# An attention, MLP and routed-expert kernel: the current token's term on TensorE, the key products on VectorE, the routing's counts one gap later

## The chip, the cores and the metric

The kernel runs on one core of a Trainium2 chip. The metric is the device time of one execution in microseconds (us): a median over runs without the profiler.

## What is computed

Three parts follow one another: an attention with a decaying state, an MLP with a squared ReLU, and a layer of 8 experts of which each token takes the best one, up to a capacity. B=2, H=8, S=768, D=48; so 1536 tokens of 384 numbers, all in float32.

```python
for t in range(S):                                   # attention, per (batch, head)
    cur = einsum('bhd,bhe->bhde', u[None] * kt, vt)  # the current token's term
    y[:, :, t] = einsum('bhd,bhde->bhe', rt, state + cur)
    state = wt[..., None] * state + einsum('bhd,bhe->bhde', kt, vt)
x = y as (tokens, 384)
x = square(maximum(x @ w_in, 0)) @ w_out             # MLP, d_ff = 2048
logits = x @ w_gate                                  # routing to 8 experts
expert, gate = argmax(logits), softmax(logits) at the argmax
slot = number of earlier tokens with the same expert # dropped if slot >= 384
out = gate * (maximum(x @ w1[expert], 0) @ w2[expert])
```

The term `cur` gives each token t and head h the vector v[t] times one number, the sum over d of r[t,d] * u[d] * k[t,d]. This sum is what the change computes in another way.

## The kernel before

**Attention** (function `attention`, class `Chunk`). The tokens go in 12 chunks of 128; chunks 0 to 5 are the first batch, 6 to 11 the second. Within a chunk, the heads go as four pairs: w, k and r lie with the head dimensions on the partitions (two heads of 48, each padded to 64) and 4 x 128 tokens along the row. v lies with the tokens on the partitions. The methods of a chunk, in the order of the mathematics:

- `suffix` (line 256) and `prefix` (276): scans of the decays on VectorE, from the chunk's end and from its start; `total` (270, 271) sets the prefix scan's first element.
- `keys` (264) multiplies k with the suffix scan, `queries` (282) r with the prefix scan. Which engine does it is set by chunk in the tables `KEYS_V` (2, 3, 4, 8 on VectorE) and `QUERIES_V` (0, 3, 6), the others on GpSimd.
- `scores` (330): 8 matmuls, `causal` (338): two masks on VectorE that read them from PSUM. `turn_keys` (292): transposes and a copy on ScalarE; `outer` (346): the chunk's addition to the state; `state` (356 or 358): two sums on VectorE; `decay` (301): the state scaled, on ScalarE.
- `values` (364, 365, 368): 12 matmuls into one PSUM tile (8 in chunks 0 and 6).
- The current token's term: `load_b` loads k and r a second time, in token order (tokens on the partitions); `bonus1` (308, 309): two products on GpSimd, k * u * r; `bonus2` (314): a reduce over each head on VectorE; `bonus3` (322): GpSimd multiplies v with the sums, into y.
- `finish` (374) adds the values to y on VectorE; `turn` (384, 385) transposes y and ScalarE rounds it to `xhi`, `turn2` (388) forms the remainder `xlo` on VectorE. `check1` and `check2` are squares on ScalarE whose sums watch for overflow.

The order of the work is written out by hand: the tuple `order` lists pairs (offset, method), and round n of the loop (`for n in range(13)`) calls the method on chunk n + offset. Each engine then works through its instructions in this order. A round so holds `total` and `prefix` of chunk n+1, `suffix` and `keys` of chunk n+2, `causal`, `outer`, `state` and `values` of chunk n, `finish` and `turn` of chunk n-1. At the end of a round the loads are issued on SP's queue: w and k of chunk n+4, the others of chunk n+3. In rounds 9 to 11 the entry `conv` starts the conversion of the MLP's weights (class `Conv`; line 122 is GpSimd's part).

**MLP** (`moe1`). It runs twice: over token groups 0 and 1 (512 tokens each), then over group 2. Each float32 product is three matmuls of rounded parts (hi*hi, hi*lo, lo*hi). Step i of its loop is up (475, 9 matmuls), the square of step i-1 (481, 482), the parts of step i-2 (488, 490), then one piece of a background generator, here called a gap, then down of step i-3 (502, 9 matmuls).

**Routing** (`route_bg`). In the gaps of the second pass groups 0 and 1 are routed: four items with the logits of 128 tokens each (578), one with `choose` (591 to 600: argmax and softmax), one with `count` and `total` (605 to 610, 633, 634: matmuls that count earlier tokens of the same expert), one with `slots`, `gates` and the first `send` (619 to 628, 656: the token's row to its expert's slot in DRAM), then three more with a `send` each. `pairs` joins two items to a gap. `judge` and `early` follow (fetch and turn the first rows of expert 0, 734 and 742). The experts come last (`experts`).

Of the kernel before, what the change touches and what calls it, by code (L numbers as in the profile page):

```python
# [19 lines left out]
P = 128  # L20
# [17 lines left out]
KEYS_V = (2, 3, 4, 8)  # L38
QUERIES_V = (0, 3, 6)
# [4 lines left out]
def tile_rwkv_moe_moe2(ctx, tc, cap, rt, kt, wt, vp, rn, kn, un, wmoe, we, wg, cf, ci, fill, vt, up, ind, out, disp, xt):  # L44
# [14 lines left out]
    ub = cpool.tile([P, DM], F32, name="ub")  # L59
# [147 lines left out]
    def attention(conv):  # L207
# [7 lines left out]
        nc.vector.memset(z1, 0.0)  # L215
        st = ap1.tile([P, NPAIR, 96], F32, name="st")
# [3 lines left out]
        class Chunk:  # L220
# [25 lines left out]
            def load_b(self):  # L246
                n = self.n
                self.kn = ap2.tile([P, DM], F32, name=f"kn_{n}", tag="kn")
                nc.sync.dma_start(self.kn, kn[n * P : (n + 1) * P, :])
                self.rn = ap2.tile([P, DM], F32, name=f"rn_{n}", tag="rn")  # L250
                nc.sync.dma_start(self.rn, rn[n * P : (n + 1) * P, :])

# [65 lines left out]
            def bonus3(self):  # L318
                self.y = ylast if self.n == 11 else ap2.tile([P, NPAIR, 2, D], F32, name=f"y_{self.n}", tag="y")
# [72 lines left out]
        def do(n, *names):  # L392
# [8 lines left out]
            "ub": lambda: nc.sync.dma_start(ub, un),  # L401
# [544 lines left out]
    def run(fast):  # L946
# [163 lines left out]
```

## Time and profile before

| | us |
|---|---|
| median of 3 runs | 474.16 |
| lowest and highest | 473.64, 476.53 |
| the profiled execution | 478.65 |
| its span, first to last instruction | 476.8 |
| TensorE busy in the span | 437.2 |
| VectorE busy | 317.0 |
| ScalarE busy | 232.7 |
| GpSimd busy | 171.1 |

PE is TensorE's matmuls, DVE VectorE, ACT ScalarE, POOL GpSimd, SP the engine whose queue issues most DMAs. Ends of matmuls are modelled, so the distance between starts says more than a duration; a float32 matmul shows as two records. In rows in order of time the first number is the start in us from the span's start, the second the us of the piece, then engine, line, operation, output<-inputs, and in brackets the idle time of the engine before it and what ended it. In rows of windows the granted clock is a share of 2.4 GHz.

### The profile page before, as it was taken

The page shows a single profiled execution, that of the slowest core. Times are in us where ns is not written, and L with a number is a line of the kernel's source. Part 1 is how long each engine was busy: PE and PEld are TensorE (multiplying, and loading weights), DVE is VectorE, ACT ScalarE, POOL GpSimd, SP SyncE. Part 2 cuts the span into 40 slices and gives each one's busy share as a digit, 9 for nine tenths or more (in the row PEclk, how much of TensorE's full clock was granted, in tenths as well). Part 3 has the DMA queues.
Part 4 walks back from the last instruction along what each step waited for, and adds up shares of the span by engine and source line. Part 5 has one row for each costly group of instructions (what it writes and reads, how often), then busy time and mean ns, then how long its engine had stood idle before and what let it go on. Part 6 is the DMA issues. An engine that isn't in the chain of part 4 may idle for free. (4 is left out here: it accounts for less than half of the span.)

```text
span 476.8 us, 7070 instructions
## 1 busy us (share of the span) xinstructions
PE 437.2 (92%) x2349; PEld 368.7 (77%) x2349; DVE 317.0 (66%) x550; ACT 232.7 (49%) x477; POOL 171.1 (36%) x174
## 2 busy tenths in 40 slices
PE   3898889799999999999989999998999889989992
PEld 2797778678888888888878787786888778878882
DVE  6989999968766667765444556532279994993230
ACT  2454445656665555663343644442357663643230
POOL 3747767723212222211004260132046662561000
PEclk9989889989999999999999999998999999999998
DMA  8775766659774232333003245416139999500000
GB/s 286 251 209 200 230 203 215 212 173 329 237 239 135 87 89 90 99 101 100 1 0 100 67 133 183 133 45 221 40 94 376 308 352 335 199 6 29 16 19 16
DMA packets 35908, 73.45 MB, mean 154 GB/s; under 512 B 3884, under 2 KB 18270, under 8 KB 35728
## 3 DMA queue, kind: packets, MB, share of 16 engines
q1 hardware_dynamic: 32336, 61.02, 39.6%
q10 hardware_dynamic: 1856, 7.33, 4.4%
q0 software_dynamic: 1664, 4.47, 2.5%
q8 instruction: 25, 0.41, 0.3%
q14 instruction: 27, 0.22, 0.1%
HBM read 68.33 MB, written 12.46 MB: 169 GB/s over the span
## 5 line engine op out<-in xcount | busy, mean ns | idle before, releaser
L490 DVE TENSOR_TENSOR glo<-gg,ghi 128x512 fp32r<-128x512 f32 x48 | 35.8, 745 | 48.4 <-ACT ghi L488 48.3
L122 POOL TENSOR_TENSOR raw<-raw 128x384 int32<-128x384 int32 x32 | 30.0, 938 | 96.6 <-ACT gg L481 77.9
L488 ACT ACTIVATE ghi<-gg 128x512 fp32r<-128x512 f32 x48 | 30.3, 632 | 60.9 <-PE px L502 60.6
L774 ACT ACTIVATE place_lo<-pu 128x512 f32<-128x512 f32 x28 | 16.7, 598 | 61.2 <-PE pu L769 61.2
L808 POOL DMA_INDIRECT out_dram<-yo,drow x13 | 16.1, 1241 | 77.1 <-DVE yo L807 44.6
L785 DVE TENSOR_TENSOR place_lo<-ph,place_hi 128x512 fp32r<-128x512 f32 x28 | 18.8, 687 | 36.4 <-ACT place_hi L784 36.4
L482 DVE SCALAR_TENSOR_TENSOR gg<-ph,gg 128x512 f32<-128x512 f32 x48 | 32.9, 685 | 14.7 <-ACT gg L481 14.7
L481 ACT ACTIVATE gg<-ph 128x512 f32<-128x512 f32 x48 | 28.7, 598 | 15.8 <-PE ph L475 11.6
L365 PE MATMUL py<-v,am 128*128 128x96 f32 x96 | 22.3, 319 | 6.8 <-DVE am L338 6.8
L365 PEld LDWEIGHTS py<-v,am 128*128 128x128 f32 x96 | 17.5, 227 | 8.0 <-DVE am L338 8.0
L368 PE MATMUL py<-v,am 128*128 128x96 f32 x96 | 22.5, 322 | 1.2
L652 POOL COPY row<-sm 128x1 f32<-128x1 f32 x9 | 2.3, 256 | 58.8 <-DVE sm L628 43.4
L769 PE MATMUL pu<-e_0hi,dhi 128*128 128x512 f32 x42 | 17.6, 420 | 3.2 <-PEq L834 2.5
L802 PE MATMUL py<-e_2hi,place_hi 128*128 128x384 f32 x56 | 20.2, 361 | 0.0
L368 PEld LDWEIGHTS py<-v,am 128*128 128x128 f32 x96 | 17.7, 230 | 2.7 <-DVE am L338 2.7
L807 DVE TENSOR_SCALAR yo<-py,drow 128x384 f32<-128x384 f32 x13 | 8.0, 613 | 17.6 <-PE py L802 17.6
L256 DVE TENSOR_TENSOR_SCAN q<-w,d1r 128x516 f32<-128x516 f32 x12 | 17.6, 1468 | 2.6 <-DMA w<-wt_dram 2.6
L116 DVE SCALAR_TENSOR_TENSOR raw<-raw,cy 128x384 int32<-128x384 int32 x32 | 18.6, 581 | 1.2
L784 ACT ACTIVATE place_hi<-ph 128x512 fp32r<-128x512 f32 x28 | 16.7, 596 | 5.0 <-ACT place_hi L784 4.7
L802 PE MATMUL py<-e_2lo,place_hi 128*128 128x384 f32 x56 | 18.9, 337 | 0.0
L802 PE MATMUL py<-e_3lo,place_hi 128*128 128x384 f32 x56 | 18.8, 336 | 0.0
L802 PE MATMUL py<-e_3hi,place_hi 128*128 128x384 f32 x56 | 18.8, 336 | 0.0
(227 smaller groups left out, 1374.8 us busy)
## 6 DMA issues: line engine op xcount, KB each, us to landing
rawe<-we_dram SPq DMA_DIRECT2D x40, 384.0 KB, 4.9
raw<-wmoe_dram SPq DMA_DIRECT2D x32, 384.0 KB, 4.0
disp_dram<-fill_dram ACTq DMA_DIRECT2D x8, 606.2 KB, 5.6
place_hi<-we_dram SPq DMA_DIRECT2D x12, 384.0 KB, 8.1
v<-vp_dram SPq DMA_DIRECT2D x12, 288.0 KB, 5.1
drow<-disp_dram SPq DMA_DIRECT2D x8, 388.0 KB, 4.1
w<-wt_dram SPq DMA_DIRECT2D x12, 258.5 KB, 4.3
k<-kt_dram SPq DMA_DIRECT2D x12, 256.0 KB, 4.7
```

The costliest lines, as they stand in the source:

```text
L116: nc.vector.scalar_tensor_tensor(raw[:, :, 1], raw[:, :, 1], -0x40000000, yi, op0=ALU.bitwise_and, op1=ALU.bitwise_or)
L122: nc.gpsimd.tensor_tensor(raw[:, :, 1], raw[:, :, 1], raw[:, :, 0], op=ALU.add)
L256: nc.vector.tensor_tensor_scan(q[:, ::-1], self.w[:, NSEG * SEG : 0 : -1], d1r[:, ::-1], 0.0, op0=ALU.mult, op1=ALU.add)
L365: nc.tensor.matmul(py[:, a, :], self.at[0][:, a, :], self.vv[:, a, 0:96], start=self.first, stop=False)
L368: nc.tensor.matmul(py[:, a, :], self.at[1][:, a, :], self.vv[:, a, 48:144], start=False, stop=True)
L481: nc.scalar.activation(gg, gh[f, g], AF.Relu)
L482: nc.vector.scalar_tensor_tensor(gg, gh[f, g], 0.0, gg, op0=ALU.max, op1=ALU.mult)
L488: nc.scalar.activation(ghi, gg, AF.Copy)
L490: nc.vector.tensor_tensor(glo, gg, ghi.bitcast(F32), op=ALU.subtract)
L769: nc.tensor.matmul(p_, xx[:, kk, :], wx[:, kk, :], start=n == 0, stop=n == 8)
L785: nc.vector.tensor_tensor(hlo, p_, hhi.bitcast(F32), op=ALU.subtract)
L802: nc.tensor.matmul(py, hx[f // 4][xi][:, f % 4, :], wx, start=n == 0, stop=n == 23)
```

## The change

1. The current token's sums. `load_b` goes. GpSimd's `bonus1` is one product z = k * r in the layout of the pairs, made one round earlier (at offset 2). `bonus2` is four matmuls on TensorE (128x128 by 128x96) of z with `ub`, which now holds u on the diagonal blocks of the pairs, so that each head's sum comes out 48 times; ScalarE copies it to y, and `bonus3` is GpSimd's product of y with v. It stands behind `bonus2`, ahead of `outer`.
2. All `keys` are on VectorE; all `queries` but chunk 0's are on GpSimd.
3. `ub` is built by ScalarE from `upt` (4 numbers a partition) instead of being loaded; the slow variant `recurrence` no longer loads `upt` itself.
4. `pairs` ends a gap after every even item instead of after every odd one: the gaps hold logits 0; logits 1 and 2; logits 3 with `choose`; `count` with `slots` and the first send; and so on.

```diff
-KEYS_V = (2, 3, 4, 8)
-QUERIES_V = (0, 3, 6)
+QUERIES_V = (0,)
...
-            def load_b(self):
-                n = self.n
-                self.kn = ap2.tile([P, DM], F32, name=f"kn_{n}", tag="kn")
-                nc.sync.dma_start(self.kn, kn[n * P : (n + 1) * P, :])
-                self.rn = ap2.tile([P, DM], F32, name=f"rn_{n}", tag="rn")
-                nc.sync.dma_start(self.rn, rn[n * P : (n + 1) * P, :])
...
             def keys(self):
-                eng = nc.vector if self.n in KEYS_V else nc.gpsimd
-                eng.tensor_tensor(self.kh, self.k, self.q3[:, :, 1:SEG], op=ALU.mult)
+                nc.vector.tensor_tensor(self.kh, self.k, self.q3[:, :, 1:SEG], op=ALU.mult)
...
             def bonus1(self):
-                nc.gpsimd.tensor_tensor(self.kn, self.kn, ub, op=ALU.mult)
-                nc.gpsimd.tensor_tensor(self.kn, self.kn, self.rn, op=ALU.mult)
+                self.z = ap2.tile([P, NPAIR, P], F32, name=f"z_{self.n}", tag="z", bufs=3)
+                nc.gpsimd.tensor_tensor(self.z, self.k, self.r, op=ALU.mult)
 
             def bonus2(self):
-                n = self.n
-                self.bs = ap2.tile([P, H], F32, name=f"bs_{n}", tag="bs")
-                nc.vector.tensor_reduce(
-                    self.bs, self.kn.rearrange("p (h d) -> p h d", d=D), op=ALU.add, axis=AX.X
-                )
+                self.pb = ps.tile([P, NPAIR, 2, D], F32, name=f"pb_{self.n}", tag="misc", bufs=3)
+                for a in range(NPAIR):
+                    nc.tensor.matmul(
+                        self.pb[:, a].rearrange("p j d -> p (j d)"), self.z[:, a, :],
+                        ub[:, a].rearrange("p j d -> p (j d)"), start=True, stop=True,
+                    )
+                self.y = ylast if self.n == 11 else ap2.tile([P, NPAIR, 2, D], F32, name=f"y_{self.n}", tag="y")
+                nc.scalar.activation(self.y, self.pb, AF.Copy)
 
             def bonus3(self):
-                bsb = self.bs.rearrange("p (a j) -> p a j", j=2).unsqueeze(3).to_broadcast([P, NPAIR, 2, D])
-                nc.gpsimd.tensor_tensor(self.y, vnat, bsb, op=ALU.mult)
+                nc.gpsimd.tensor_tensor(self.y, self.y, vnat, op=ALU.mult)
...
-            (1, "total"), (0, "scores"), (-1, "finish"), (1, "turn_keys"), (1, "prefix"), (0, "causal"), (2, "suffix"), (1, "queries"), (0, "bonus2"), (0, "outer"), (2, "keys"), (-1, "turn"), (1, "check1"), (0, "state"), (0, "bonus3"), (1, "bonus1"), (1, "decay"), (0, "conv"), (0, "values"), (-1, "turn2"), (1, "check2"),
+            (1, "total"), (0, "scores"), (-1, "finish"), (1, "turn_keys"), (1, "prefix"), (0, "causal"), (2, "suffix"), (1, "queries"), (0, "bonus2"), (0, "bonus3"), (0, "outer"), (2, "keys"), (2, "bonus1"), (-1, "turn"), (1, "check1"), (0, "state"), (1, "decay"), (0, "conv"), (0, "values"), (-1, "turn2"), (1, "check2"),
...
-            do(n + 3, "load_r", "load_v", "load_b")
+            do(n + 3, "load_r", "load_v")
...
             for i, _ in enumerate(g_):
-                if i % 2:
+                if i % 2 == 0:
                     yield
```

VectorE's instructions of round 9, before; pl, p and q are the scale, the prefix scan and the suffix scan, kh the keys, am the masked scores, bs the sums of the current token, st the state, xlo the remainder of the output.

```order
L270 TENSOR_SCALAR pl_10_898<-q_845 128x4
L271 RECIPROCAL z_93<-pl_10_898 128x4
L374 TENSOR_TENSOR y_866<-py_875,y_866 128x384
L276 SCALAR_TENSOR_TENSOR p_919<-w_716,z_93 128x516
L338 TENSOR_TENSOR am_0_921<-psc_0_901,cst 128x512
L338 TENSOR_TENSOR am_1_923<-psc_1_902,cst 128x512
L256 SCALAR_TENSOR_TENSOR q_925<-w_800,d1r 128x516
L314 TENSOR_REDUCE bs_929<-kn_724 128x8
L358 TENSOR_TENSOR st<-t_870,pu_931 64x4x48 x2
L388 TENSOR_TENSOR xlo_939<-pt_940,xhi_938 128x3x128
```

The same round after the change, again VectorE.

```order
L263 TENSOR_SCALAR pl_10_892<-q_839 128x4
L264 RECIPROCAL z_94<-pl_10_892 128x4
L370 TENSOR_TENSOR y_848<-py_873,y_848 128x384
L269 SCALAR_TENSOR_TENSOR p_913<-w_714,z_94 128x516
L334 TENSOR_TENSOR am_0_915<-psc_0_895,cst 128x512
L334 TENSOR_TENSOR am_1_917<-psc_1_896,cst 128x512
L250 SCALAR_TENSOR_TENSOR q_919<-w_798,d1r 128x516
L257 TENSOR_TENSOR kh_936<-k_800,q_919 128x512
L354 TENSOR_TENSOR st<-t_868,pu_931 64x4x48 x2
L384 TENSOR_TENSOR xlo_941<-pt_942,xhi_940 128x3x128
```

The reduce into bs is gone from its place behind the suffix scan, and the key product stands there.

GpSimd's instructions of round 9 before: the query product (rh), the key product (kh), y of chunk 9 and the two products of the bonus of chunk 10 (kn).

```order
L282 TENSOR_TENSOR rh_927<-p_919,r_804 128x512
L264 TENSOR_TENSOR kh_936<-k_802,q_925 128x512
L322 TENSOR_TENSOR y_948<-v_722,bs_929 128x384
L308 TENSOR_TENSOR kn_808<-kn_808,ub 128x384
L309 TENSOR_TENSOR kn_808<-kn_808,rn_810 128x384
```

GpSimd after the change, from the z of round 8 to the query product of round 10.

```order
L303 TENSOR_TENSOR z_858<-k_716,r_802 128x512
L275 TENSOR_TENSOR rh_921<-p_913,r_802 128x512
L318 TENSOR_TENSOR y_928<-y_928,v_720 128x384
L303 TENSOR_TENSOR z_938<-k_800,r_888 128x512
L275 TENSOR_TENSOR rh_994<-p_988,r_888 128x512
```

A round now has three products: the queries, then y with v, then z of the chunk after the next.

TensorE in the second pass of the MLP before, around the counts (pp) of group 0; pr are the logits, ph and px the up and down products.

```order
L578 MATMUL pr_2_2361<-idg,place_hi_2250 128x136 x3
L578 MATMUL pr_3_2370<-idg,place_hi_2250 128x136 x3
...
L475 MATMUL ph_3_2379<-xlo_939,m0hi 128x512
L475 MATMUL ph_3_2379<-xhi_938,m0lo 128x512 x3
L605 LDWEIGHTS upre
L605 MATMUL pp_2406<-oh_2252,upre 128x32
L606 LDWEIGHTS ones
L606 MATMUL pp_2406<-ohc,ones 128x32
```

After the change, from the last logits of group 0 to the first of the counts.

```order
L579 MATMUL pr_3_2391<-idg,place_hi_2254 128x136 x3
...
L503 MATMUL px_0_2410<-ghi_0_2352,m8hi 128x512
...
L476 MATMUL ph_4_2422<-xlo_941,m2hi 128x512
L476 MATMUL ph_4_2422<-xhi_940,m2lo 128x512 x3
L606 LDWEIGHTS upre
L606 MATMUL pp_2439<-oh_2256,upre 128x32
```

Between the last logits and the counts there were 9 up matmuls; now there are 9 down and 9 up matmuls, and the choice is made between them.

## Rows read from the trace of the kernel before

**Rows 1.** Busy us by engine in two stretches; last: granted clock, DMA share, GB/s.

```profile
10.00:84.30 74.30, 65.12 (x529) 59.82 (x527) 70.33 (x116) 33.72 (x94) 52.22 (x47) 0.91 0.70 224
100.10:300.00 199.90, 197.11 (x879) 158.18 (x878) 127.77 (x267) 109.80 (x220) 46.49 (x65) 1.00 0.41 127
```

**Rows 2.** VectorE in order of time, round 9: start us, us, instruction.

```profile
75.97 0.55 DVE L270 TENSOR_SCALAR pl<-q 128x4 f32<-128x4 f32 x1
...
76.65 0.54 DVE L374 TENSOR_TENSOR y<-py,y 128x384 f32<-128x384 f32 x1
77.11 1.44 DVE L276 TENSOR_TENSOR_SCAN p<-w,z 128x516 f32<-128x516 f32 x1
78.47 1.26 DVE L338 TENSOR_TENSOR am<-psc,cst 128x512 f32<-128x512 f32 x2
79.65 1.92 DVE L256 TENSOR_TENSOR_SCAN q<-w,d1r 128x516 f32<-128x516 f32 x1
81.50 0.52 DVE L314 TENSOR_REDUCE bs<-kn 128x8 f32<-128x384 f32 x1
81.94 0.70 DVE L358 TENSOR_TENSOR st<-t,pu 64x192 f32<-64x192 f32 x2
82.67 0.56 DVE L388 TENSOR_TENSOR xlo<-pt,xhi 128x384 fp32r<-128x384 f32 x1
...
84.29 1.45 DVE L276 TENSOR_TENSOR_SCAN p<-w,z 128x516 f32<-128x516 f32 x1
```

**Rows 3.** The scan of line 256: shortest, median, longest.

```profile
L256 DVE TENSOR_TENSOR_SCAN q<-w,d1r x12: 1215/1301/1934, 3.6 to 79.7; 128x516 f32<-128x516 f32 x12
```

**Rows 4.** GpSimd in order of time, 14 to 80 us.

```profile
14.87 1.75 POOL L322 TENSOR_TENSOR y<-v,bs 128x384 f32<-128x384 f32 x1
...
79.30 1.18 POOL L282 TENSOR_TENSOR rh<-p,r 128x512 f32<-128x512 f32 x1
```

**Rows 5.** VectorE in order of time, 13.8 to 19 us.

```profile
13.81 0.55 DVE L314 TENSOR_REDUCE bs<-kn 128x8 f32<-128x384 f32 x1 [0.73 <-POOL kn L309]
14.28 1.72 DVE L256 TENSOR_TENSOR_SCAN q<-w,d1r 128x516 f32<-128x516 f32 x1
16.04 1.14 DVE L264 TENSOR_TENSOR kh<-k,q 128x512 f32<-128x512 f32 x1
...
18.99 1.23 DVE L276 TENSOR_TENSOR_SCAN p<-w,z 128x516 f32<-128x516 f32 x1
```

**Rows 6.** TensorE in order of time, round 9; a matmul is two records.

```profile
75.63 1.16 PE L330 MATMUL psc<-rh,kh 64*128 64x128 f32 x16
...
77.21 1.03 PE L346 MATMUL pu<-v,kts 128*128 128x96 f32 x8
78.08 0.49 PE L384 MATMUL pt<-cst,y 128*128 128x128 f32 x3
...
80.08 0.39 PE L364 MATMUL py<-t,rh 128*128 128x96 f32 x2
...
81.87 0.39 PE L368 MATMUL py<-v,am 128*128 128x96 f32 x2
```

**Rows 7.** TensorE in order of time, end of attention.

```profile
92.14 0.55 PE L384 MATMUL pt<-cst,y 128*128 128x128 f32 x3 [1.62 <-DVE y L374]
...
97.63 0.77 PE L475 MATMUL ph<-xhi,m0hi 128*128 128x512 f32 x1
```

**Rows 8.** Four stretches at the lower clock: the last, and all together.

```profile
93.20:100.00 6.80, 6.67 (x26) 6.18 (x27) 5.02 (x12) 2.77 (x7) 1.89 (x2) 0.50 0.22 60
sum 20.40, PE 20.27 PEld 19.22 DVE 16.91 ACT 8.63 POOL 10.78; mean PE 5.07 PEld 4.80 DVE 4.23 ACT 2.16 POOL 2.69
```

**Rows 9.** TensorE in order of time, second expert pass, 245.9 to 273 us.

```profile
247.45 0.19 PE L605 MATMUL pp<-oh,upre 128*128 128x32 bf16 x1 [1.51 <-ACT sm L600]
...
272.17 0.19 PE L605 MATMUL pp<-oh,upre 128*128 128x32 bf16 x1 [0.57 <-ACT sm L600]
```

**Rows 10.** DMA issues: KB each, median us to landing.

```profile
r<-rt_dram SPq DMA_DIRECT2D x12, 256.0 KB, 4.9
```

More of the change, by code (lines that the diff above doesn't have):

```diff
@@ L58, in tile_rwkv_moe_moe2 @@
     cid = cpool.tile([P, 12], I32, name="cid")
-    ub = cpool.tile([P, DM], F32, name="ub")
+    upt = cpool.tile([P, NPAIR], F32, name="upt")
+    ub = cpool.tile([P, NPAIR, 2, D], F32, name="ub")
     idg = cpool.tile([P, KT, P + NE], F32, name="idg")
@@ L215, in attention @@
         nc.vector.memset(z1, 0.0)
+        nc.gpsimd.memset(ub, 0.0)
         st = ap1.tile([P, NPAIR, 96], F32, name="st")
@@ L307, in bonus1 @@
             def bonus1(self):
-                nc.gpsimd.tensor_tensor(self.kn, self.kn, ub, op=ALU.mult)
-                nc.gpsimd.tensor_tensor(self.kn, self.kn, self.rn, op=ALU.mult)
+                self.z = ap2.tile([P, NPAIR, P], F32, name=f"z_{self.n}", tag="z", bufs=3)
+                nc.gpsimd.tensor_tensor(self.z, self.k, self.r, op=ALU.mult)
             def bonus2(self):
-                n = self.n
-                self.bs = ap2.tile([P, H], F32, name=f"bs_{n}", tag="bs")
-                nc.vector.tensor_reduce(
-                    self.bs, self.kn.rearrange("p (h d) -> p h d", d=D), op=ALU.add, axis=AX.X
-                )
+                self.pb = ps.tile([P, NPAIR, 2, D], F32, name=f"pb_{self.n}", tag="misc", bufs=3)
[6 more added lines that the diff above has]
+                nc.scalar.activation(self.y, self.pb, AF.Copy)
             def bonus3(self):
-                self.y = ylast if self.n == 11 else ap2.tile([P, NPAIR, 2, D], F32, name=f"y_{self.n}", tag="y")
                 vnat = self.vv.rearrange("p a (j d) -> p a j d", d=D)[:, :, 0:3:2, :]
-                bsb = self.bs.rearrange("p (a j) -> p a j", j=2).unsqueeze(3).to_broadcast([P, NPAIR, 2, D])
-                nc.gpsimd.tensor_tensor(self.y, vnat, bsb, op=ALU.mult)
+                nc.gpsimd.tensor_tensor(self.y, self.y, vnat, op=ALU.mult)
             def scores(self):
@@ L400, in attention @@
             "cst": lambda: nc.sync.dma_start(cst, cf),
-            "ub": lambda: nc.sync.dma_start(ub, un),
+            "ub": lambda: nc.sync.dma_start(upt, up),
         }
         for n, name in (
-            (0, "load_w"), (0, "load_k"), (0, "load_r"), (0, "cst"), (0, "load_b"), (1, "load_w"), (0, "ub"), (1, "load_k"), (2, "load_w"), (0, "load_v"), (1, "load_r"), (1, "load_v"), (2, "load_k"), (2, "load_r"), (2, "load_b"), (1, "load_b"), (3, "load_w"), (3, "load_k"), (2, "load_v"),
+            (0, "load_w"), (0, "load_k"), (0, "load_r"), (0, "cst"), (0, "ub"), (1, "load_w"), (1, "load_k"), (2, "load_w"), (0, "load_v"), (1, "load_r"), (1, "load_v"), (2, "load_k"), (2, "load_r"), (3, "load_w"), (3, "load_k"), (2, "load_v"),
         ):
@@ L411, in attention @@
         do(1, "suffix", "keys")
+        for j in range(2):
+            hs = slice(64 * j, 64 * (j + 1))
+            nc.scalar.activation(ub[hs, :, j, :], upt[hs].unsqueeze(2).to_broadcast([64, NPAIR, D]), AF.Copy)
         do(0, "bonus1", "check1", "decay", "check2")
         order = (
-            (1, "total"), (0, "scores"), (-1, "finish"), (1, "turn_keys"), (1, "prefix"), (0, "causal"), (2, "suffix"), (1, "queries"), (0, "bonus2"), (0, "outer"), (2, "keys"), (-1, "turn"), (1, "check1"), (0, "state"), (0, "bonus3"), (1, "bonus1"), (1, "decay"), (0, "conv"), (0, "values"), (-1, "turn2"), (1, "check2"),
+            (1, "total"), (0, "scores"), (-1, "finish"), (1, "turn_keys"), (1, "prefix"), (0, "causal"), (2, "suffix"), (1, "queries"), (0, "bonus2"), (0, "bonus3"), (0, "outer"), (2, "keys"), (2, "bonus1"), (-1, "turn"), (1, "check1"), (0, "state"), (1, "decay"), (0, "conv"), (0, "values"), (-1, "turn2"), (1, "check2"),
         )
@@ L424, in attention @@
                         do(0, "bonus2")
+                    if (n, o, name) == (0, 1, "queries"):
+                        do(1, "bonus1")
                 elif 12 - LEAD <= n < 12:
@@ L880, in recurrence @@
         nc.sync.dma_start(indt, ind)
-        upt = sp.tile([P, NPAIR], F32, name="upt")
-        nc.sync.dma_start(upt, up)
         st_ = [sp.tile([P, B, S + 1], F32, name=f"sst_{i}") for i in range(2)]
```

## The prediction

> **What bounds the kernel now.** I read the busy time by stage first. In attention's middle VectorE is busy 70.33 of 74.3 us, TensorE 65.12 at a mean clock of 0.91, GpSimd 52.22, ScalarE 33.72; from 100 to 300 us, in the matrix layer and its routing, TensorE is busy 197.11 of 199.9 us [rows 1]. So VectorE sets the pace of attention, TensorE that of what follows, and each microsecond by which attention ends earlier should reach the end of the program.
>
> Next, VectorE in order of time through round 9 (the loop over n) [rows 2]. It never rests: scale (line 270), finish, prefix scan, two masks, suffix scan, bonus reduce, two state sums, remainder; from one prefix scan to the next 84.29 - 77.11 = 7.18 us. Over rounds 2 to 10 the mean is (84.29 - 18.99) / 9 = 7.26 us [rows 2, 5]. Part of that is waiting inside instructions. The suffix scan took 1.92 us here, and its durations go from 1.215 to 1.934 [rows 3]: it began at 79.65 while GpSimd's query product ran from 79.30 to 80.48 [rows 4], and did its own 1.1 us after that. The other way round, GpSimd's product at 14.87 (1.75 us) lay behind the scan that ended at 16.00, ran 0.62 us until 16.62, and the key product that VectorE issued at 16.04 ended at 17.18 [rows 4, 5]. They take turns: whoever waits gets the next turn, and the other's next instruction waits.
>
> The Trainium skill (SBUF — State Buffer, "SBUF: two separate sides") says the same: a VectorE instruction with two SBUF inputs and a GpSimd instruction that reads SBUF exclude each other for the whole instruction. These rows agree. The rule speaks against a part of this change, which gives VectorE such an instruction in every round: by it a round comes to the 6.98 us of the sum below, and if the two shared instead, to TensorE's 6.4.
>
> TensorE in round 9 [rows 6], at 2.4 GHz: scores and key transposes 1.58 us (75.63 to 77.21), outer product 0.87, output transposes 0.33, values 12 matmuls at (81.87 - 80.08) / 8 = 0.224, that is 2.7: in all 5.5 us of 7.2. At the lower clock all of that doubles. The four stretches at the lower level (0.50, so 1.2 GHz) make 20.4 us [rows 8]; the last runs from 93.2 to 100.0, and before it TensorE had stood idle 1.62 us for the finish of chunk 10 [rows 7].
>
> **The change, part by part.**
>
> Start, up to the prefix scan of chunk 2 at 18.99. The reduce of chunk 0 goes, 0.47 us from its start to the next, with the wait of 0.73 before it [rows 5]; the key products of chunks 0 and 1 come, 2 x 0.56; GpSimd's first z, ready once r has landed, stands in the way of one scan, and two products of its bonus no longer stand in the way of another. These nearly cancel: I take -0.35 us, bounds -1.8 and +1.
>
> Rounds 2 to 10. From round 9's 7.18 us these go: the reduce, 0.44 from its start to the next [rows 2]; the suffix scan's wait, 1.92 against the median 1.30 [rows 2, 3], since the query product now starts right behind the prefix scan with nothing of GpSimd's queued before it: 0.62; the prefix scan's wait, 1.44 against 1.23 [rows 2, 5]: 0.2; and of the 0.68 from the scale to finish 0.3, an estimate, for the GpSimd product that then ran beside it. This comes: the key product, in four chunks on VectorE before and in all now. The one at 16.04 took 1.14 us, of which 0.56 after its turn came, so 0.6 is its own [rows 4, 5]. And a new collision: GpSimd's y product is ready behind the query product, waits for the suffix scan, and gets its turn before the key product. It reads two full tiles, so it runs 0.62 us [rows 4, 5] to 1.0; I take 0.76. Sum: 7.18 - 0.44 - 0.62 - 0.2 - 0.3 + 0.6 + 0.76 = 6.98 us. Then z has its turn behind the keys, some 1.0 us, beside the state sums and the remainder, which read PSUM, and ends about as the next round's scale starts. Nine rounds: 9 x 6.98 = 62.8 against 65.3, so -2.5 us. Bounds: with no collision the round is 6.2 on VectorE, but TensorE holds it at 6.4 (below), -7.5; with z late on top of the y collision +8 (a rival below). Two query products leave VectorE too; the round of the sum has none, so they are in it.
>
> TensorE gets four matmuls a chunk of the form of line 346, 128x128 by 128x96: 0.87 us a round, so 5.5 + 0.87 = 6.4 at 2.4 GHz, still under 6.98. It hides, with 0.6 us to spare, and it fills the time in which TensorE waited for the masks. If that cover is gone, at 1.2 GHz, a round takes 12.7 us of TensorE. ScalarE's new copy, one a chunk, hides in an engine busy less than half [rows 1]; GpSimd's y needs it, and the copy is done while the query product still runs.
>
> End of attention, from the prefix scan of chunk 11 at 84.29. Before: 13.34 us to the first matmul of the matrix layer at 97.63 [rows 2, 7], and 2.4 us more at 1.2 GHz, which lose 1.2. After, step by step: the scan itself 1.23, masks of chunk 10 1.18, its values 2.7, scores of chunk 11 1.16, its four new matmuls 0.87, output transposes 0.33, by when the masks of chunk 11 are made, and its values 2.7: in all 10.2, and I take 10.5. The reduces of chunks 10 and 11 are gone, and GpSimd's two products of chunk 11, which ran beside the weight conversion, were replaced by one, two rounds earlier. TensorE then has no gap like the 1.62 us, so I take the clock to stay at 2.4 GHz: -(13.34 + 1.2 - 10.5) = -4.0 us. Bounds: -0.5 (lower clock as before) and -4.5.
>
> The Trainium skill (TensorE: Matmul & The Clock Gate, "HAM oscillation — how this bites in real kernels") has matmuls that pause for others fall back to the lower clock, round after round. By this rule a TensorE that is fed throughout keeps the clock; the trace agrees as far as the stretch behind the 1.62 us gap goes.
>
> Loads. The rows of k and r in token order, 24 loads of 192 KB, leave SP's queue, with the waits for the reduce that stood ahead of the next weights. But k of chunk n+4 now waits for z of n+2, and r of n+3 is queued behind it and needed a round earlier, by z: issued at 0.4 us of the next round, landing 4.9 us later [rows 10], at 5.3, needed at 5.9. It just hides.
>
> Routing, second pass of the matrix layer. Counting stands behind the choice in one gap, and TensorE waits for it 1.51 us and 0.57 us [rows 9]. Moved one gap later, the choice is done a whole step (18 matmuls) before. In the same gap VectorE's slots now wait for the counts; behind them stands the square of the next tile, which has a step to spare. The rows are sent in the same gap as before. -2.1 us; bounds 0 and -2.3.
>
> Sum: -0.35 - 2.5 - 4.0 - 2.1 = -9.0 us. This is of the profiled execution, 478.65 us (span 476.8 and 1.85 around it), 4.5 above the median of the runs shown, 474.16. Taken off the median: 465.2 us.
>
> **Rivals.**
>
> The collisions don't come (keys win the turn, z fits in): TensorE's 6.4 becomes the round. 9 x 0.86 = 7.7 less than 65.3: sum -14.2, 460.0 us. For it: two engines could fall into a better rhythm. Against: GpSimd's y is ready too early for that.
>
> The clock: the stretches at 1.2 GHz stay. Then TensorE sets the rounds touched, the round stays at 7.26 and the end gains 0.5: -0.35 - 0.5 - 2.1 = -3.0, 471.2 us. For it: 20.4 us in the trace [rows 8], and only 0.6 us of slack where there were 1.7. Against: the gaps ahead of these stretches shrink.
>
> Slower: z is late. Its r lands after the y product, z runs beside the next scale and prefix scan instead of beside the state sums, and VectorE waits its 1.18 us (as the query product, of the same form [rows 4]) in each round: 8.16 us, 9 x 8.16 = 73.4, +8.1; the clock falls as before, end -0.5, start -0.35, routing -2.1: +5.2, 479.4 us. It decides from a round of 8.1 us up. For it: a margin of 0.6 us. Against: the transfers that r competes with lose a quarter of their bytes.
>
> The routing's wait only moves to the slots and the sends: -6.9, 467.3 us.
>
> **How the numbers follow.** Forecast 0.56, own range 462 to 469; no collisions 0.14; clock 0.19; z late 0.05; routing 0.06. About 1% (4.7 us) is what a measurement of this kernel can tell from no change. Faster by over 1%: nearly all of the forecast and of the first rival, most of the last, a fifth of the clock's: 0.77. Slower: z late, 0.05. Same: the rest, 0.18. The range goes from 460.5, near the first rival, to 472.5, past the clock's.
>
> **What would show it.** Right: prefix scans 7.0 us apart; keys on VectorE near 1.3 us, with y just ended; suffix scans near 1.3; scale near 0.2; the clock at 2.4 GHz from about 28 us on; the first matmul of the matrix layer near 91 us; no idle time before the counts. Wrong: prefix scans 7.3 us apart or more, or the idle gap before the output transposes of chunk 10 still there with the lower clock behind it; a z that ends after the next scale begins; a new gap of TensorE at the first expert's rows.

## The result, and the profile after

The changed kernel takes 468.45 us (median of 4 runs, 466.89 to 468.99), the kernel before 474.25 in the same comparison: a ratio of 0.9846, 95% interval 0.9813 to 0.9879. Taken again in a later batch (e10, below) the ratio is 0.9827, interval 0.979 to 0.9863. So the change gains 1.5 and 1.7% in the two batches. Forecast were 465.2 us, that is 1.9%, in a range of 460.5 to 472.5. The profiled execution took 468.99 us, its span 467.2.

Windows by stage after the change (columns: stretch, us, busy us of TensorE, its weight loads, VectorE, ScalarE, GpSimd, then granted clock, DMA share, GB/s); it answers to [rows 1] and, in the second row, to [rows 8].

```profile
10.00:84.30 74.30, 70.22 (x632) 64.84 (x628) 72.71 (x116) 39.21 (x110) 50.10 (x33) 1.00 0.58 186
```

```profile
14.30:318.00 303.70, 296.39 (x1706) 249.07 (x1705) 216.73 (x427) 166.14 (x372) 107.82 (x116) 1.00 0.44 138
```

TensorE, at 65.12 busy us before, stands at 70.22 of 74.3, nearly as full as VectorE (72.71), and from 14.3 to 318 us its clock never leaves 2.4 GHz. The stretches of [rows 8] in attention are gone.

VectorE in order of time through one round after the change; it answers to [rows 2]. Line 250 is the suffix scan, 257 the keys, 269 the prefix scan.

```profile
74.27 0.16 DVE L263 TENSOR_SCALAR pl<-q 128x4 f32<-128x4 f32 x1
...
75.01 1.22 DVE L269 TENSOR_TENSOR_SCAN p<-w,z 128x516 f32<-128x516 f32 x1
76.15 1.26 DVE L334 TENSOR_TENSOR am<-psc,cst 128x512 f32<-128x512 f32 x2
77.33 1.34 DVE L250 TENSOR_TENSOR_SCAN q<-w,d1r 128x516 f32<-128x516 f32 x1
78.71 1.30 DVE L257 TENSOR_TENSOR kh<-k,q 128x512 f32<-128x512 f32 x1
79.94 0.71 DVE L354 TENSOR_TENSOR st<-t,pu 64x192 f32<-64x192 f32 x2
80.67 0.56 DVE L384 TENSOR_TENSOR xlo<-pt,xhi 128x384 fp32r<-128x384 f32 x1
81.15 0.16 DVE L263 TENSOR_SCALAR pl<-q 128x4 f32<-128x4 f32 x1
...
81.90 1.22 DVE L269 TENSOR_TENSOR_SCAN p<-w,z 128x516 f32<-128x516 f32 x1
```

GpSimd in the same round; it answers to the second row of [rows 4].

```profile
76.41 1.18 POOL L275 TENSOR_TENSOR rh<-p,r 128x512 f32<-128x512 f32 x1 [2.12 <-DMA r<-rt_dram]
77.54 1.92 POOL L318 TENSOR_TENSOR y<-y,v 128x384 f32<-128x384 f32 x1
79.42 1.73 POOL L303 TENSOR_TENSOR z<-k,r 128x512 f32<-128x512 f32 x1
```

The turns can be read off the ends. The suffix scan ends at 78.67; y, issued at 77.54, does its own work then and ends at 79.46; the keys, issued at 78.71, do theirs from there and end at 80.01; z, issued at 79.42, does its own from there and ends at 81.15, at the very moment the scale starts. The round is 81.90 - 75.01 = 6.89 us, 7.18 before [rows 2]. Seven of the nine rounds from the prefix scan of chunk 2 on take 6.8 to 6.9 us, the other two 7.3.

VectorE at the start after the change, then GpSimd; they answer to [rows 5] and the first row of [rows 4]. Line 435 is a conversion to bf16.

```profile
14.63 1.59 DVE L257 TENSOR_TENSOR kh<-k,q 128x512 f32<-128x512 f32 x1
...
17.08 1.43 DVE L435 CAST ohc<-cst 128x8 bf16<-128x8 f32 x1
...
19.23 1.22 DVE L269 TENSOR_TENSOR_SCAN p<-w,z 128x516 f32<-128x516 f32 x1
```

```profile
13.45 2.21 POOL L303 TENSOR_TENSOR z<-k,r 128x512 f32<-128x512 f32 x1
...
17.04 1.29 POOL L303 TENSOR_TENSOR z<-k,r 128x512 f32<-128x512 f32 x1
```

The keys of chunk 2 (1.59 us) wait for the first of these z, which ends at 15.66, the conversion (1.43) for the second, which ends at 18.33.

TensorE at attention's end and in the routing after the change; the rows answer to [rows 7] and [rows 9].

```profile
88.81 0.49 PE L380 MATMUL pt<-cst,y 128*128 128x128 f32 x3
...
91.74 0.48 PE L476 MATMUL ph<-xhi,m0hi 128*128 128x512 f32 x1
...
266.08 0.19 PE L606 MATMUL pp<-oh,upre 128*128 128x32 bf16 x1
...
266.97 0.18 PE L673 MATMUL p<-ohc,ones 128*128 128x1 bf16 x1 [0.60 <-ACT gg L482]
```

The idle 1.62 us before the output transposes of chunk 10 are gone, and from the last prefix scan to the first MLP matmul it is now 91.74 - 81.90 = 9.84 us. The counts (line 606) no longer wait. A small matmul of the padding count (line 673) waits instead, 0.60 us, once. At the first expert's rows TensorE waits 1.6 us, 1.4 before: no new gap.

In the two profiled executions, 476.8 - 467.2 = 9.6 us went like this: up to the prefix scan of chunk 2, 19.23 against 18.99, +0.24; the nine rounds from there, (81.90 - 19.23) = 62.67 against 65.30, -2.63; the end of attention, 9.84 against 13.34 and 1.2 for the lower clock, -4.7; the routing, 0.60 against 1.51 + 0.57, -1.48. These make -8.6; the other 1.0 lies behind the first MLP matmul and was not traced to a place.

### The profile page after: what moved, and what is told of

Read it like the earlier page. It is cut to its first block, busy times and chain, and to the rows that moved or that the text cites. A ratio compares the mean times of both kernels' runs of the same rounds, so it can differ in the third digit from the quotient of the medians.

```text
span 467.2 us, 7230 instructions
## 1 busy us (share of the span) xinstructions
PE 436.0 (93%) x2445; PEld 370.5 (79%) x2445; DVE 314.4 (67%) x544; ACT 237.5 (51%) x491; POOL 165.2 (35%) x157
## 5 line engine op out<-in xcount | busy, mean ns | idle before, releaser
L275 POOL TENSOR_TENSOR rh<-p,r 128x512 f32<-128x512 f32 x11 | 13.0, 1186 | 27.3 <-DVE p L269 20.2
L294 ACT ACTIVATE t<-st,q 128x96 f32<-128x96 f32 x40 | 11.7, 363 | 20.9 <-DVE st L354 16.3
L361 PE MATMUL py<-v,am 128*128 128x96 f32 x96 | 19.3, 283 | 2.8 <-DVE am L334 2.8
L303 POOL TENSOR_TENSOR z<-k,r 128x512 f32<-128x512 f32 x12 | 20.4, 1704 | 3.5 <-DMA r<-rt_dram 3.5
L364 PE MATMUL py<-v,am 128*128 128x96 f32 x96 | 19.3, 283 | 1.4
L318 POOL TENSOR_TENSOR y<-y,v 128x384 f32<-128x384 f32 x11 | 19.7, 1795 | 0.0
```

The lines of the kernel that those rows point to most:

```text
L303: nc.gpsimd.tensor_tensor(self.z, self.k, self.r, op=ALU.mult)
L318: nc.gpsimd.tensor_tensor(self.y, self.y, vnat, op=ALU.mult)
L361: nc.tensor.matmul(py[:, a, :], self.at[0][:, a, :], self.vv[:, a, 0:96], start=self.first, stop=False)
L364: nc.tensor.matmul(py[:, a, :], self.at[1][:, a, :], self.vv[:, a, 48:144], start=False, stop=True)
```

## The experiments

All twelve kernels beside the kernel before of their batch. The median of before was 475.57 us for e1 to e4, 474.94 for e5 to e8, 476.12 for e9 to e11 and 476.46 for e12.

| | kernel | median us | ratio to before, 95% interval | granted clock, median |
|---|---|---|---|---|
| e1 | before + pairs | 473.57 | 0.9961, 0.9941 to 0.9981 | 0.980 |
| e2 | after, old pairs | 470.27 | 0.9892, 0.9873 to 0.9912 | 0.992 |
| e3 | before + keys on VectorE | 475.55 | 0.9999, 0.9981 to 1.0018 | 0.979 |
| e4 | before + sums on TensorE | 469.71 | 0.9883, 0.9862 to 0.9903 | 0.994 |
| e5 | before + matmuls nobody reads | 474.02 | 0.9968, 0.9947 to 0.9989 | 0.991 |
| e6 | after, state first | 469.80 | 0.9885, 0.9853 to 0.9917 | 0.993 |
| e7 | after + a fourth product | 480.39 | 1.0105, 1.0055 to 1.0156 | 0.980 |
| e8 | after + a memset | 476.66 | 1.0029, 1.0007 to 1.005 | 0.984 |
| e9 | after, keys behind the state | 465.43 | 0.9784, 0.9745 to 0.9823 | 0.991 |
| e10 | after | 467.62 | 0.9827, 0.979 to 0.9863 | 0.994 |
| e11 | after, keys on GpSimd | 464.58 | 0.9766, 0.9729 to 0.9803 | 0.995 |
| e12 | e9 with e11's start | 463.44 | 0.9722, 0.9689 to 0.9755 | 0.995 |

**e1: the pairs alone,** in the kernel before.

```diff
-                if i % 2:
+                if i % 2 == 0:
```

> The kernel before with the routing's gaps alone changed (count one gap later). Theory (TensorE's wait for the choice is lost time): the waits of 1.51 and 0.57 us before the counts go, 0.6 us comes back before the single matmul of the padding (as in the changed kernel's trace), so the time falls by 1.5 us, 474.2 to 472.7. Rival (the wait only moves to the slots and sends, or is made up later): no change, 474.2 within 0.4.

Measured 473.57, 2.0 us less than before of its batch. TensorE in order of time shows what is left of the waits of [rows 9]:

```profile
271.74 0.18 PE L672 MATMUL p<-ohc,ones 128*128 128x1 bf16 x1 [0.55 <-DVE ohc L634]
```

The counts themselves start without idle time; behind them one matmul waits 0.55 us for VectorE's totals (line 634). So the edit gives 1.5 us of waits and about that in the time: a part that adds to the others.

**e2: the change with the old pairs,** an edit of the changed kernel.

```diff
-                if i % 2 == 0:
+                if i % 2:
```

> The changed kernel with the old gaps of the routing. Theory: 1.5 us slower than the changed kernel, 468.45 to 470.0, with idle times of about 1.5 and 0.6 us before the counts. Rival: no change, 468.5.

Measured 470.27; the waits are back, 1.54 and 0.60 us:

```profile
239.95 0.19 PE L606 MATMUL pp<-oh,upre 128*128 128x32 bf16 x1 [1.54 <-ACT sm L601]
```

**e3: all keys on VectorE, all queries but chunk 0's on GpSimd, in the kernel before.**

```diff
-KEYS_V = (2, 3, 4, 8)
-QUERIES_V = (0, 3, 6)
+KEYS_V = tuple(range(12))
+QUERIES_V = (0,)
```

> The kernel before with only the tables changed: all keys on VectorE, queries of chunks 3 and 6 on GpSimd; the current token's term as before. Theory (a key product on VectorE costs its own 0.6 us and a turn of GpSimd): eight more key products at 0.6 to 1.2 us, two query products fewer at 0.6, less the relief of a round whose GpSimd work falls by 1.2: rounds of 7.5 to 7.9 us, 3 us slower than before, 477. Rival (GpSimd's load, not VectorE's, holds the rounds): the relief pays for it, 474 or less.

Measured no difference, 0.9999: neither the 3 us more of the theory nor the 474 of its rival. VectorE in one round, then GpSimd's y beside it:

```profile
75.94 0.53 DVE L270 TENSOR_SCALAR pl<-q 128x4 f32<-128x4 f32 x1
76.51 0.18 DVE L271 RECIPROCAL z<-pl 128x4 f32<-128x4 f32 x1
...
77.06 1.55 DVE L276 TENSOR_TENSOR_SCAN p<-w,z 128x516 f32<-128x516 f32 x1
...
81.39 0.68 DVE L264 TENSOR_TENSOR kh<-k,q 128x512 f32<-128x512 f32 x1
```

```profile
81.55 1.21 POOL L322 TENSOR_TENSOR y<-v,bs 128x384 f32<-128x384 f32 x1 [1.61 <-DVE bs L314]
```

The keys cost VectorE 0.68 us here and wait for nothing, since y of the kernel before waits for the reduce that stands ahead of them; the suffix scan stays at 1.31. But the prefix scan still waits for the second product of the bonus (1.55), and the scale for the first (0.53). The round stays at 7.28 us (84.34 - 77.06): the row on VectorE changes its parts and keeps its length.

**e4: the sums on TensorE alone,** written as an edit of the changed kernel.

```diff
-QUERIES_V = (0,)
+KEYS_V = (2, 3, 4, 8)
+QUERIES_V = (0, 3, 6)
...
-                nc.vector.tensor_tensor(self.kh, self.k, self.q3[:, :, 1:SEG], op=ALU.mult)
+                eng = nc.vector if self.n in KEYS_V else nc.gpsimd
+                eng.tensor_tensor(self.kh, self.k, self.q3[:, :, 1:SEG], op=ALU.mult)
...
-                if i % 2 == 0:
+                if i % 2:
```

> The changed kernel with the old tables for keys (2, 3, 4 and 8 on VectorE) and queries (0, 3 and 6), and the old gaps: of the change the current token's sums on TensorE alone. Theory (VectorE's round is its own work plus turns of GpSimd): keys on GpSimd put four products in its round, and the last of them, z, runs into the next scale and prefix scan; rounds near 7.0, and with the old gaps 470 to 471. Rival (the sums on TensorE and the reduce that goes are all of the gain, keys on VectorE only cost): faster than the changed kernel with the old gaps, rounds near 6.5, 466.

Measured 469.71, just under the 470 to 471 of the theory and far from its rival's 466. Against e2, which has the same pairs and all keys on VectorE, 470.27: moving the keys from the old tables to VectorE brings nothing. VectorE in rounds whose keys and queries are GpSimd's:

```profile
72.60 0.84 DVE L265 TENSOR_SCALAR pl<-q 128x4 f32<-128x4 f32 x1
73.48 0.18 DVE L266 RECIPROCAL z<-pl 128x4 f32<-128x4 f32 x1
...
74.03 1.74 DVE L271 TENSOR_TENSOR_SCAN p<-w,z 128x516 f32<-128x516 f32 x1
...
80.76 1.74 DVE L271 TENSOR_TENSOR_SCAN p<-w,z 128x516 f32<-128x516 f32 x1
```

GpSimd beside it:

```profile
72.24 1.18 POOL L259 TENSOR_TENSOR kh<-k,q 128x512 f32<-128x512 f32 x1
73.38 1.30 POOL L305 TENSOR_TENSOR z<-k,r 128x512 f32<-128x512 f32 x1
```

A round is 80.76 - 74.03 = 6.73 us, although the scale now waits for the end of GpSimd's keys (73.42) and the prefix scan for that of z (74.68). The reciprocal between them runs beside z and waits for nothing. The four rounds with keys or queries on VectorE took 6.87, 8.35, 6.30 and 7.41 us in the same execution, and all nine 6.83 on average, against 6.96 (62.67 / 9) in the changed kernel. The sums on TensorE are all of attention's gain. How that gain divides among the reduce, GpSimd's product and the 24 loads that go with them was not tested apart.

**e5: four matmuls a round that nobody reads, in the kernel before.** They stand in `bonus2` and fill TensorE where the changed kernel has its new matmuls.

```diff
+                px_ = ps.tile([P, NPAIR, 96], F32, name=f"px_{n}", tag="misc", bufs=3)
+                for a in range(NPAIR):
+                    nc.tensor.matmul(px_[:, a, :], ident, ub[:, 96 * a : 96 * (a + 1)], start=True, stop=True)
```

> The kernel before with four more matmuls a round (identity by 128x96 numbers, into a PSUM tile that nobody reads), at the place where the changed kernel has its four. Theory (part of the gain is the clock: TensorE without its idle times keeps 2.4 GHz): rounds as before, the idle times before the masked products shrink by up to 0.87 us, the mean granted clock of the runs rises from 0.979 to about 0.99, and the time falls by 2 to 4 us although work was added: 472 to 473.5 against 475.5. Rival (the clock follows from the faster rounds, or does not matter): time as before or slower, clock 0.98.

Measured 474.02, 0.9 us less than before of its batch (0.32%, interval 0.11 to 0.53), not the 2 to 4 us of the theory, although the clock rose as it had it. Windows of this kernel: attention, its one stretch at half the clock there, and the end of attention, in the columns of [rows 1].

```profile
10.00:84.30 74.30, 68.98 (x615) 64.42 (x613) 71.69 (x119) 34.18 (x95) 53.82 (x48) 0.98 0.71 229
52.34:55.75 3.41, 3.41 (x26) 3.24 (x24) 2.80 (x7) 1.34 (x4) 3.33 (x4) 0.50 0.45 128
92.00:100.00 8.00, 7.75 (x48) 6.34 (x46) 6.75 (x15) 5.20 (x12) 2.91 (x3) 1.00 0.42 125
```

The mean clock rises from 0.978 to 0.991, that of the changed kernel, and of the stretches of [rows 8] this one is left. The nine rounds take 7.14 us on average, 7.26 before, since VectorE sets them. So on the medians the clock alone is worth about 1 us (0.5 to 2.5 by the interval) of the 5.8 and 8.5 us that the changed kernel gains: most of that gain is not its clock.

In the one execution of before that was traced the clock cost more. TensorE at the end of attention, in e5:

```profile
91.64 0.55 PE L387 MATMUL pt<-cst,y 128*128 128x128 f32 x3 [0.55 <-DVE y L377]
...
95.08 0.48 PE L478 MATMUL ph<-xhi,m0hi 128*128 128x512 f32 x1
```

The last prefix scan starts at 83.78. From it to the output transposes it is 7.86 us, as before (92.14 - 84.29 = 7.85); to the first MLP matmul it is 11.30, against 13.34 and 1.2 more behind it [rows 7, 8]. Behind the transposes both kernels have the same instructions and only the clock differs, so 13.34 + 1.2 - 11.30 = 3.2 of the 4.7 us by which the end of attention shrank are the lower clock of that execution; the other 11.30 - 9.84 = 1.5 us are the change's own.

The Trainium skill (TensorE: Matmul & The Clock Gate, "HAM oscillation — how this bites in real kernels") blames pauses between groups of matmuls for the lower clock. The clocks agree with it, 0.978 against 0.991; the time shows that a lower clock costs little where TensorE waits for another engine anyway (7.26 against 7.14 us a round), and much where TensorE alone is waited for (3.2 us at the end of attention).

**e6: the state's sums and the total ahead of the keys,** in the tuple `order` of the changed kernel. The state's sums read PSUM; y was to run beside them instead of holding up the keys.

```diff
-        do(1, "suffix", "keys")
+        do(1, "suffix", "total", "keys")
...
-            (1, "total"), (0, "scores"), (-1, "finish"), ...
+            (0, "scores"), (-1, "finish"), ...
...
-            ... (0, "outer"), (2, "keys"), (2, "bonus1"), (-1, "turn"), (1, "check1"), (0, "state"), ...
+            ... (0, "outer"), (-1, "turn"), (1, "check1"), (0, "state"), (2, "total"), (2, "keys"), (2, "bonus1"), ...
```

> The changed kernel with VectorE's round in another order: the state sums right behind the suffix scan, then the scale of the next prefix scan, then the keys. Theory (the key product loses 0.6 us a round because GpSimd's y takes its turn behind the suffix scan; sums that read PSUM need no turn): keys near 0.69 us instead of 1.30, y beside the state sums, z beside remainder and finish, rounds of 6.3 to 6.5 us at TensorE's own 6.4, 9 rounds 3 to 5 us shorter: 464 to 465.5. Rival (the turn only moves to the scale or the prefix scan, or TensorE already holds the rounds): rounds 6.8 to 6.9, 468.5.

Measured 469.8; the rounds are 7.24 us, 0.36 longer than the changed kernel's, outside theory and rival. GpSimd, then VectorE, in order of time:

```profile
64.66 1.93 POOL L318 TENSOR_TENSOR y<-y,v 128x384 f32<-128x384 f32 x1
66.55 1.29 POOL L303 TENSOR_TENSOR z<-k,r 128x512 f32<-128x512 f32 x1
```

```profile
65.71 0.69 DVE L354 TENSOR_TENSOR st<-t,pu 64x192 f32<-64x192 f32 x2
66.44 0.17 DVE L263 TENSOR_SCALAR pl<-q 128x4 f32<-128x4 f32 x1
...
66.74 1.65 DVE L257 TENSOR_TENSOR kh<-k,q 128x512 f32<-128x512 f32 x1
```

y did run beside the state's sums. But the keys came at 66.74, 0.15 us behind the end of y (66.59), and by then z had begun: 1.65 us instead of 1.30. The scale and the reciprocal had stood between the state and the keys. Who is not there when the other ends loses the turn.

**e7: a second z that nobody reads,** behind the first in `bonus1` of the changed kernel.

```diff
+                zz = ap2.tile([P, NPAIR, P], F32, name=f"zz_{self.n}", tag="zz", bufs=1)
+                nc.gpsimd.tensor_tensor(zz, self.k, self.r, op=ALU.mult)
```

> The changed kernel in which GpSimd makes z a second time, into a tile that nobody reads, right behind the first. GpSimd is idle for 2.1 us in each round and would have room for it. Theory (turns): the second product runs beside the next scale and prefix scan, VectorE waits for it, rounds 7.7 to 8.1 us, time 8 to 11 us longer, 477 to 480. Rival (GpSimd's idle time hides it): rounds 6.9, 468.5.

Measured 480.39, just above the theory's range. VectorE's scale pays all of it:

```profile
74.78 1.29 DVE L263 TENSOR_SCALAR pl<-q 128x4 f32<-128x4 f32 x1
```

1.29 against 0.16, and the round 8.00 against 6.88 us (78.98 - 70.98 from one suffix scan to the next). GpSimd stands idle 2 us a round ahead of the queries, yet that hides nothing: z ends just as the scale starts, so what is put behind z falls on VectorE.

**e8: a memset of GpSimd in the same place,** which reads nothing.

```diff
+                zz = ap2.tile([P, 2, NPAIR, P], F32, name=f"zz_{self.n}", tag="zz", bufs=1)
+                nc.gpsimd.memset(zz, 0.0)
```

> As the run with the fourth product, but GpSimd fills a tile of 128x1024 with zeros instead (about 1 us, it reads no SBUF). Theory (turns are taken for reads of SBUF alone): VectorE's scans and keys do not wait for it; only the scale, which has one input, may; rounds 6.9 to 7.0, time 468.5 to 469.5. Rival (any GpSimd instruction that touches SBUF takes a turn, or GpSimd's load itself counts): rounds 7.6 or more, 476 or more.

Measured 476.66, rounds of 7.64 us. GpSimd, then VectorE:

```profile
73.31 0.95 POOL L305 MEMSET zz<- 128x1024 f32 x1
```

```profile
73.34 0.94 DVE L263 TENSOR_SCALAR pl<-q 128x4 f32<-128x4 f32 x1
```

The theory's time was wrong: the scale, with 4 columns and one input, which "may" wait, waits for the whole of a memset that only writes, 0.78 us a round. No scan and no key product came while the memset ran, so whether those wait for an instruction that reads nothing wasn't tried.

The Trainium skill (SBUF — State Buffer, "SBUF: two separate sides") lets a VectorE instruction with two SBUF inputs wait only for a GpSimd instruction that reads SBUF. The scale has one input and waits; what the page has for that is a VectorE instruction in one of the modes that use both port pairs, and no row here shows an instruction's mode. The reciprocal of e4, as small and with one input too, did not wait for z.

**e9: the state's sums ahead of the keys, and the scale behind the next finish,** in `order` of the changed kernel: e6 without what came between.

```diff
-            (1, "total"), (0, "scores"), (-1, "finish"), (1, "turn_keys"), ...
+            (0, "scores"), (-1, "finish"), (1, "total"), (1, "turn_keys"), ...
...
-            ... (0, "outer"), (2, "keys"), (2, "bonus1"), (-1, "turn"), (1, "check1"), (0, "state"), ...
+            ... (0, "outer"), (-1, "turn"), (1, "check1"), (0, "state"), (2, "keys"), (2, "bonus1"), ...
```

> The changed kernel with VectorE's order in a round rewritten: the state's addition and the two products around it ahead of the keys, and the total's scaling behind the finish of the next round, so that GpSimd's y would run beside the state's addition, the keys would stand ready (own time 0.6 us) when y gives up its turn, and z would run beside what follows. Theory (an engine that waits gets the next turn, and the state's addition takes none): keys 0.6 to 0.7 us instead of 1.30, the total's scaling 0.16, the prefix scan 1.22, rounds of 6.3 to 6.5 us instead of 6.88, 9 to 10 of them, 464 to 466 us against about 468.5 of the changed kernel. Rival (the turn only moves, or TensorE's own 6.4 us of work a round and its waits bound the round): rounds of 6.8 to 7.3 us, 468 us or more.

Measured 465.43, against 467.62 of the changed kernel in the same batch (e10). VectorE, then GpSimd, in one round:

```profile
54.56 1.34 DVE L250 TENSOR_TENSOR_SCAN q<-w,d1r 128x516 f32<-128x516 f32 x1
55.83 0.70 DVE L352 COPY st<-pu 64x192 f32<-64x192 f32 x2
56.56 0.69 DVE L257 TENSOR_TENSOR kh<-k,q 128x512 f32<-128x512 f32 x1
...
58.22 0.22 DVE L263 TENSOR_SCALAR pl<-q 128x4 f32<-128x4 f32 x1
```

```profile
54.77 1.93 POOL L318 TENSOR_TENSOR y<-y,v 128x384 f32<-128x384 f32 x1
56.66 1.75 POOL L303 TENSOR_TENSOR z<-k,r 128x512 f32<-128x512 f32 x1
```

Now the keys are there at 56.56, before y ends at 56.70, and z waits for them, not they for z: 0.69 us instead of 1.30. z runs beside the remainder and the finish and ends at 58.41, when the scale has lost 0.06. The rounds are 6.53 us, a little over the 6.3 to 6.5 of the theory, and the first MLP matmul starts at 88.6 us instead of 91.7. Both engines are full: VectorE is busy 50.42 of the 52 us from 26 to 78, and TensorE's longest gap from 22 us to the first MLP matmul is 0.39 us.

**e10: the changed kernel again.**

> The changed kernel unchanged, for a comparison in the same batch. By every theory 468 to 469 us, rounds of 6.88 us, first MLP matmul at 91.7 us.

Measured 467.62 (466.94 to 468.72), 8.5 us less than before of its batch.

**e11: the keys of chunks 2 to 11 back on GpSimd,** in the changed kernel.

```diff
-                nc.vector.tensor_tensor(self.kh, self.k, self.q3[:, :, 1:SEG], op=ALU.mult)
+                (nc.vector if self.n < 2 else nc.gpsimd).tensor_tensor(self.kh, self.k, self.q3[:, :, 1:SEG], op=ALU.mult)
```

> The changed kernel with the keys of chunks 2 to 11 by GpSimd, which then has four or five products a round. Theory (the sums by TensorE are all of the gain, and the rounds of e4 whose keys and queries were GpSimd's were 6.7 us long although their scaling and prefix scan waited for z): rounds of about 6.7 us, so 9 x 0.18 = 1.6 us less than the changed kernel, 466 to 468 us. Rival (keys on VectorE are a part of the gain: GpSimd's row gets too long, as where a fourth product of no use was added): rounds of 7.5 us or more, 474 us or more.

Measured 464.58, 3.0 us less than e10. VectorE at the start and in a late round:

```profile
17.69 1.41 DVE L269 TENSOR_TENSOR_SCAN p<-w,z 128x516 f32<-128x516 f32 x1
...
58.02 1.74 DVE L269 TENSOR_TENSOR_SCAN p<-w,z 128x516 f32<-128x516 f32 x1
```

Most rounds are 6.7 us long, as the theory had it, and the start is 1.54 us shorter (17.69 against 19.23), which it had not: the keys of chunk 2 no longer stand behind GpSimd's z there. Not all of the 1.54 is shown to be the keys': e12 runs the same instructions up to that scan and starts it at 18.86. The first MLP matmul is at 88.6 us. So keys of chunks 2 to 11 on VectorE cost 3 us against the same keys on GpSimd. The kernel before had four of them on VectorE; against that mixture they cost nothing that shows (e4 and e2, 0.6 us).

**e12: e9 with the changed kernel's order in rounds 0 and 1** (the tuple `first`; `late` is e9's) **and chunk 2's keys on GpSimd.**

```diff
-        order = (
+        first = (
...
+        late = (
...
-            for o, name in order:
+            for o, name in first if n < 2 else late:
...
-                nc.vector.tensor_tensor(self.kh, self.k, self.q3[:, :, 1:SEG], op=ALU.mult)
+                (nc.gpsimd if self.n == 2 else nc.vector).tensor_tensor(self.kh, self.k, self.q3[:, :, 1:SEG], op=ALU.mult)
```

> The kernel of e9 with two things of e11's start: the order of the changed kernel for rounds 0 and 1 and the keys of chunk 2 by GpSimd, so that the prefix scan of chunk 2 starts at 17.7 us instead of 19.57. Theory (attention is now TensorE's: e9 and e11 both reach the first MLP matmul at 88.6 us, with 1.4 and 1.8 us of gaps of TensorE behind 9 us left in all): the earlier start removes the 1.0 us gap at 20.4 us and no more, first MLP matmul at 87.5 to 88.2 us, 464 to 465.2 us. Rival (rounds still hang on VectorE's chain, which starts 1.9 us earlier): first MLP matmul at 86.7 us, 463 us or less. If the early rounds collide instead: 466 us.

Measured 463.44, but not by either reason given. The prefix scan of chunk 2 starts at 18.86 us, 0.7 earlier than in e9, not 1.9; the next rounds are 7.3 and 6.95 us; the first MLP matmul comes at 89.0, 0.5 later than in e9. Three of e9's six executions had a clock of 0.987 or 0.988 and took 466.2 us or more, the others 0.994 and up and 464.05 to 464.63; all of e12's had 0.995 and up. So about half of the 2 us between the two medians lies in executions of e9 with more of the lower clock (its other three have a median of 464.44); where the other 1.0 comes from is not shown, and the early start gained nothing in the traced execution. One of e12's six executions took 1099.43 us; it has no trace, and whether the slow variant of attention ran in it stays open. So e9 and e11 are the versions to go by.

## Why the prediction was right, and where it was off

**What bounds the kernel: right.** VectorE set attention's pace and TensorE what follows. In the two traces the whole 4.7 us at the end of attention and the 2.63 of the rounds arrived at the end of the program.

**Start: wrong, and small.** Forecast -0.35, measured +0.24. I had set the collisions off against each other; in fact GpSimd's z products hold up the keys of chunk 2 (1.59 us) and a conversion (1.43). The keys on VectorE are a part of the cause: with chunk 2's on GpSimd the start is 1.54 us shorter in e11, but only 0.37 in e12.

**Rounds: right, term by term, and the total helped by luck.** Forecast 9 x 6.98 = 62.8 us, measured 62.67. Seven of the rounds are 0.1 to 0.2 us shorter than forecast; two take 7.3, one because finish waits 0.32 us for TensorE, one because of a suffix scan of 1.71 behind a late query product, and the sum had neither. Keys 1.30 (0.6 of their own and 0.76 of y's turn: 1.36), suffix scan 1.34, scale 0.16, prefix scan 1.22, y just ended when the keys do their own work. The forecast of TensorE, 6.4 us a round, is what limits e9 to 6.53 beside VectorE's own row.

**End of attention: right for the traced pair.** Forecast 10.5 us at 2.4 GHz, measured 9.84; -4.7 instead of -4.0. The gap and the lower clock behind it went as forecast. But 3.2 of the 4.7 are that lower clock (e5), which is no fixed part of the kernel before: that is the term that failed below.

**The clock: right that it would stay high.** It stays at 2.4 GHz from 14.3 to 318 us, so the rival with its 471.2 us fell. e5 adds that on the medians the clock alone is worth some 1 us.

**The rival without collisions (460.0): fell** as argued, since y is ready before the keys. e9 is the nearest that an order came to it, with 6.53 us a round.

**Routing: mis-sized.** Forecast -2.1, measured -1.48 in the traces; the waits before the counts went, and 0.6 us came back one matmul later, at the padding's count. That is the rival in which the wait only moves, for a good quarter of it.

**"z late": right that it would not come, but without room to spare.** z ends as the scale starts, and in one round it was late: there the scale at 52.58 took 0.80 us. e7 and e8 show the price of coming late in every round: 1.13 and 0.78 us.

**The keys on VectorE:** I counted them as a cost of 1.36 us that the gains outweigh, and never asked what the change would be without them. e4 shows the same gain with the old tables, e11 that with the keys of chunks 2 to 11 on GpSimd it is 3 us larger.

**The step that failed: "Taken off the median".** The sum, -9.0 us, was of the profiled execution, and there it was near: -9.6 was measured, of which -8.6 in the parts named, where the misses of start and routing (+0.6 each) and of the end (-0.7) partly cancel. I then took it off 474.16. But the profiled execution of before (478.65 us, clock 0.970) was a long one with more of the lower clock than most. Of 68 executions of before in the four batches, with a median of 475.63 us and a clock of 0.977, the 12 at 0.972 or less have a median of 477.27, the 15 at 0.983 or more one of 474.27. A part of the 9.0 was the lower clock's cost in that execution, some 3 us of it at the end of attention, and a median execution has less of that to give: e5, whose traced execution is 3.3 us shorter than that one (475.33 against 478.65), is 0.9 us shorter on the median. The median of three, 474.16, was itself 1.5 us below that of the 68. Taken off the profiled time the sum gives 478.65 - 9.0 = 469.65, and the profiled execution of after took 468.99. Off the median of the 68 it gives 466.6, between the forecast and the 467.62 and 468.45 measured.

## What to carry to other kernels

Where VectorE and GpSimd take turns, read the ends of their instructions, not the starts: the engine that already waits when the other ends gets the next turn, so an instruction that needs no turn belongs between the other engine's start and the instruction that would wait for it (e9: 0.6 us off the keys, 0.36 off the round). Test each part of a change that comes in one piece: here one part held all of attention's gain, another gave nothing, and its opposite gives 3 us more (e11). And take a sum worked out from one profiled execution off that execution's time; how far its clock stands from those of the median runs says how much of the sum the median will not show.

## What the runs showed of the hardware that was not expected

A scale of 128x4 with one input waited for the whole of a GpSimd product and of a GpSimd memset: 0.16 us alone, 0.94 behind a memset of 0.95 (e8), 1.29 behind a product of 1.29 (e7); the reciprocal behind it doesn't wait (e4). And 0.15 us decide a turn: keys that come that much too late take 1.65 us (e6), keys that come 0.14 early 0.69 (e9).
